# Reordering POOL's work, two operations changing engine, and 128-row v tiles in a windowed attention followed by a gated convolution

## The chip, the cores and the metric

The kernel runs on one core of a Trainium2 chip. The metric is the device time of one execution in microseconds. Before the change the median of three runs is 299.91 us (298.84 to 300.24).

## The reference

Batch 4, 8 heads, 768 positions, head size 64, all in float32. The first half is an attention in which a query sees the keys at a distance under 16 and, besides, one summary per block of 32 keys; the second half is a causal convolution of five taps that gates a projection.

```python
k_sum = k.reshape(B, H, nb, 32, D).max(axis=3)
v_sum = v.reshape(B, H, nb, 32, D).mean(axis=3)
scores_l = where(|i - j| < 16, q @ k.T / 8, -1e9)
scores_s = q @ k_sum.T / 8 + log(32)
a = softmax(concat(scores_l, scores_s))
x = a @ concat(v, v_sum)                 # B x 768 x 512
gate = sigmoid(sum_k conv_w[k] * x shifted by k)
out = (gate * (x @ w_val)) @ w_out
```

## The kernel before

A unit is a third of one batch's positions (256, four tiles of 64 queries) and four of the heads (two pairs); a group is two units and has all 512 channels of its positions. There are 24 units and 12 groups, three groups to a batch. The order of instructions is written out by hand and is the order in which each engine gets them. `step(s)` interleaves three units: it makes the scores of unit s, transposes the probabilities of unit s - 1, and multiplies unit s - 2 with v. The first four units and part of the fifth are written out singly ahead of the loop.

What a step gives each engine, in order:

- TensorE: a product from a queue (`proj`: an output product `out_mm`, L486), `mm_x` (probabilities times v, L393), `mm_s` (scores, L317), the first half of the transpositions `tp` (L373), a second product from the queue (a value product `val_mm`, L462), the second half of `tp`. In odd steps the value product reads the `xl` that the same step makes.
- VectorE: `snorm` (scores with mask and row maxima into `sn` and `nm`, L334), `taps` (the convolution, L437, and the first product of one head pair from group 3 on, L433), the reciprocal of the sums in `norm` (L356, L357), `val_ev` (`gf`, gate times value, L472), and in some steps `prep_k` (maxima `ks` of 32 keys, L126, and two copies of them into the key tile, L136).
- ScalarE: `out_ev` (`ob`), `xout` (`xh`, the part of x that TensorE's fast float form holds, L408, and `xf`, L409), `ginit` (first product of the convolution, x times the last tap, L422), the exponentials `exps`, the copies of the transposed tiles `pcopy` (`pts`, L377), `gate` (tanh, L445), and `gh` in `val_ev`.
- POOL: `xl` = `xf` - `xh` (L411), the halo of the next group (L294), `norm`'s multiplication of `p` by 1/sum in two halves (L360), `gl` = `gf` - `gh` in `val_ev` (L474), and in some steps `prep_v`, a tree of five additions that sums blocks of 32 columns of `vT` (L147).
- SyncE issues all transfers, in order.

`xl` and `gl` are the low parts of a split: a float32 product is made as three products of the fast form, `xh` with the high and the low part of the weights and `xl` with the high part. `split_w` makes the two parts of a weight tile (ScalarE's cast L247, POOL's subtraction L248) from a staged tile that `conv_w` fills (ScalarE L207, VectorE L209 and L210). For `wo` the staged tile `wst` has two buffers for four weight tiles.

`mm_x` reads a tile `v` of 120 rows, in which rows 16 to 27 and 92 to 103 are block means. `load_v` fetches the others from memory, from group 2 on in three pieces of 16, 64 and 16 rows, two transfers each; `fill_vs` puts the block means in with four transfers of 48 KB.

The trees and key maxima of batch b are made in the steps that `PREP_V` and `PREP_K` list: for b of 2 or 3, trees in steps 6b - 4 to 6b - 1 and maxima in steps 6b - 3 to 6b. Within a step `late_loads` puts both at the end.

Of the kernel before, what the change touches and what calls it, by code (L numbers as in the profile page):

```python
# [24 lines left out]
NTH = 3  # L25
# [16 lines left out]
NP = 2 * TPU  # L42
ACT_TAP_G = 3
LOADS = "k0 q0 m k1 q1 n0 i k2 q2 n1 k3 q3 n2 n3 v0 c Q w0 w1 w2 w3 v1 o0 o1 o2 o3"
UPB = NTH * NHP
LOAD_K = {1: (2, 2, 4, 5)}
PREP_K = {1: (4, 5, 5, 6)}
PREP_V = {1: (3, 4, 5, 5)}
for _b in range(2, B):
# [6 lines left out]
def tile_attention_then_gated_conv(  # L56
# [56 lines left out]
    def load_v(g):  # L113
        b, th = divmod(g, NTH)
        t = ld.tile([KW, TPU, DM], F32, tag="v", name=f"v_{g}")
        pieces = ((0, WIN), (OFF_O, OFF_B), (OFF_N, KW)) if g > 1 else ((0, KW),)
        for r0, r1 in pieces:
            for e in range(VP):
                nc.sync.dma_start(t[r0:r1, 2 * e : 2 * e + 2], vw[b, th, e, r0:r1])
        vtile[g] = t  # L120

    def prep_k(b, pr):
        t = ktile[b, pr]
        ks = wk.tile([P, NB], F32, tag="ks", name=f"ks_{b}_{pr}")
        own = t[:, OFF_O : OFF_O + STEP * NT].rearrange("p (t c) -> p t c", c=STEP)[:, :, :QT]
        nc.vector.tensor_reduce(  # L126
            ks.rearrange("p (t j) -> p t j", j=2),
            own.rearrange("p t (j c) -> p t j c", c=BLK),
            AX.X,
            ALU.max,  # L130
        )
        for half, n in ((0, NT // 2 + 1), (1, NT // 2)):
            c0 = OFF_A + half * STEP
            dst = t[:, c0 : c0 + 2 * STEP * n].rearrange("p (t c) -> p t c", c=2 * STEP)[:, :, :HB]
            src = ks[:, half * HB : half * HB + HB]
            nc.vector.tensor_copy(dst, src.unsqueeze(1).broadcast_to([P, n, HB]))  # L136

# [241 lines left out]
    def mm_x(u):  # L379
# [5 lines left out]
        for r in range(2):  # L385
            for i in range(TPU):
                for h in range(2):
                    c0 = (2 * hp + r) * P + h * D
                    dst = xp[h * D : (h + 1) * D, r, i * QT : (i + 1) * QT]
                    src = s["pts"][  # L390
                        :, TPU * r + 2 * (i // 2) + h, (i % 2) * QT : (i % 2 + 1) * QT
                    ]
                    nc.tensor.matmul(dst, v[:, i, c0 : c0 + D], src, start=True, stop=g > 0)  # L393
                    if g == 0:
                        nc.tensor.matmul(
                            dst, vblk[i % 2][:, c0 : c0 + D], src, start=False, stop=True
                        )

    def xout(u):
# [10 lines left out]
        if g:  # L410
            nc.gpsimd.tensor_tensor(  # L411
                G["xl"][:, prs, :], x[:, prs, HALO:], G["xh"][:, prs, :].bitcast(F32), ALU.subtract
            )

    def ginit(u):
# [4 lines left out]
        gt = s["gt"] = ps_g.tile([P, 2, SG], F32, tag="g", name=f"g_{u}")  # L420
        for r in range(2 if g < ACT_TAP_G else 1):
            nc.scalar.activation(  # L422
# [3 lines left out]
    def taps(u):  # L426
# [3 lines left out]
        for r in range(2):  # L430
            pr = 2 * hp + r
            if r and g >= ACT_TAP_G:
                nc.vector.tensor_scalar(  # L433
# [31 lines left out]
    def val_ev(g, cp, pp):  # L465
        G = group(g)
        cos = slice(2 * cp, 2 * cp + 2)
        if "gh" not in G:
# [4 lines left out]
        nc.scalar.copy(G["gh"][:, cos, :], gf)  # L473
        nc.gpsimd.tensor_tensor(  # L474
            G["gl"][:, cos, :], gf, G["gh"][:, cos, :].bitcast(F32), ALU.subtract
        )

# [35 lines left out]
    def early_loads(s):  # L513
        g, hp = divmod(s, NHP)
        if hp == 0 and 1 <= g < NG - 1:
            load_q(g + 1)
        for b in range(1, B):
            for i in range(NPR):
                if s == LOAD_K[b][i]:
                    load_k(b, i)  # L520
                    load_vT(b, i)

    def late_loads(s):
        g, hp = divmod(s, NHP)
        for b in range(1, B):
            for i in range(NPR):
                if s == PREP_K[b][i]:
                    prep_k(b, i)
                if s == PREP_V[b][i]:
                    prep_v(b, i)  # L530
            if s == b * UPB:
                prep_vs(b)
                fill_vs(b * NTH)
        if hp == NHP - 1 and 1 <= g < NG - 1:
            load_v(g + 1)
            if (g + 1) % NTH:
                fill_vs(g + 1)

    def step(s, late=lambda: None):
        u, t, x = s < NU, s - 1 < NU, s - 2 < NU  # L540
# [6 lines left out]
        if x:  # L547
# [3 lines left out]
            if hp == NHP - 1:  # L551
                queue_proj(g)
                if g + 1 < NG:
                    group(g + 1)
        if u:
            mm_s(s, 0)
            mm_s(s, 1)
# [8 lines left out]
        if u:  # L566
            exps(s, 1)
        if x:
            taps(s - 2)
# [60 lines left out]
    exps(2, 1)  # L630
    group(1)
    early_loads(2)
# [7 lines left out]
    ppv = [val_mm(0, 0), val_mm(0, 1)]  # L640
    split_w("wv", 0)
    split_w("wv", 1)
    taps(0)
    gate(0)
    ginit(1)
    norm(3)
    tp(2, 0)
    pcopy(2, 0)
    val_ev(0, 0, ppv[0])
    conv_w("wo", 0)  # L650
    conv_w("wo", 1)
    taps(1)
    tp(2, 1)
    pcopy(2, 1)
    gate(1)
    early_loads(3)
    split_w("wv", 2)
    val_ev(0, 1, ppv[1])
    split_w("wv", 3)
    late_loads(3)  # L660

    def late4():
        for k in range(2):
            split_w("wo", k)
# [6 lines left out]

    step(4, late4)
    step(5, late5)
    for s in range(6, NU + 2):
        step(s)
    while queue:
        proj()()

# [5 lines left out]
def _layout(q, k, v, moe_w_val, moe_conv_w, moe_w_out):  # L684
# [10 lines left out]
    vn[:, WIN : WIN + S] = v.transpose(0, 2, 1, 3).reshape(B, S, DM)  # L695
    vw = np.zeros((B, NTH, VP, KW, 2, DM), f)
    for t in range(NT):
# [52 lines left out]
```

## Time and profile before

| | before |
|---|---|
| median of 3 runs | 299.91 us (298.84 to 300.24) |
| the profiled execution | 299.31 us |
| its span | 297.5 us |
| TensorE, VectorE, ScalarE, POOL busy | 235.7, 211.6, 185.7, 148.6 us |
| granted TensorE clock, mean | 0.935 |

The span is the part of the execution that the trace covers, from the first to the last instruction. A row of a timeline has the start in us from the start of the span, the duration, the engine, the line, the operation, what it writes and reads, and in brackets the idle time before it and what ended that. Several equal instructions in a row are merged ("x8"). Each of an engine's instructions starts when the one before it is through and its inputs are there.

### The profile page before, as it was taken

What the parts mean: (1) busy time and instruction counts of PE and PEld (TensorE: products, weight loads), DVE (VectorE), ACT (ScalarE), POOL (GpSimd) and SP (SyncE); (2) the same over time, 40 slices, a digit from 0 to 9 for tenths busy, and PEclk for the clock granted to TensorE, in tenths of its full rate; (3) what the DMA queues carried; (4) which work ended last, traced back from release to release, by engine and by line L of the source; (5) the groups of instructions that cost most, each with busy time, mean ns of one, the idle gap of its engine ahead of it and who ended that gap; (6) DMA issues with size and microseconds to landing.
All of it is one profiled execution on the core that took longest, in us unless ns stands there. A gap on an engine that the chain in (4) does not pass through costs nothing.

```text
span 297.5 us, 7371 instructions
## 1 busy us (share of the span) xinstructions
PE 235.7 (79%) x2660; PEld 202.0 (68%) x2660; DVE 211.6 (71%) x740; ACT 185.7 (62%) x603; POOL 148.6 (50%) x187
## 2 busy tenths in 40 slices
PE   1268960726798995995998977986989989989895
PEld 0147840625497884884877866866868888878783
DVE  2887976599488677599498776598488876766600
ACT  2468956927088774774676873765757897774321
POOL 1150465883935547636832565665651465443330
PEclk9999996687599997998999997997999999999999
DMA  7999898516003986836106777824105452100112
GB/s 237 380 292 306 281 338 159 221 62 170 2 35 51 259 257 173 234 103 193 40 0 143 210 255 198 245 74 148 37 12 168 124 148 60 37 2 35 37 51 90
DMA packets 16848, 43.64 MB, mean 147 GB/s; under 512 B 2988, under 2 KB 3756, under 8 KB 16812
## 3 DMA queue, kind: packets, MB, share of 16 engines
q1 hardware_dynamic: 16812, 43.18, 48.5%
q8 instruction: 21, 0.34, 0.5%
q14 instruction: 15, 0.12, 0.2%
HBM read 34.71 MB, written 6.29 MB: 138 GB/s over the span
## 4 chain that ended last, share of the span: by engine, by line
DVE 34%; PE 33%; POOL 16%; DMA 8%; ACT 4%; issue 4%; SPq 0%; POOLq 0%; DVEq 0%; ACTq 0%
DVE g L437 18%; PE out L486 14%; PE val L462 10%; DVE sn L334 6%; POOL p L360 5%; DMA raw_wv<-in_wv_dram 4%; PE x L393 4%; PE s L317 4%; POOL gl L474 3%; POOL vT L147 3%; POOL xl L411 3%; DVE k L136 2%; PE pt L373 2%; DMA k<-in_kT_dram 2%; DMA qbd<-in_qT_dram 2%
## 5 line engine op out<-in xcount | busy, mean ns | idle before, releaser
L437 DVE SCALAR_TENSOR_TENSOR g<-xf,cwt,g 128x256 f32<-128x256 f32 x192 | 93.8, 489 | 13.1 <-ACT g L422 5.7
L360 POOL TENSOR_TENSOR p<-p,ri 128x480 f32<-128x480 f32 x48 | 46.5, 991 | 88.3 <-DVE ri L357 82.1
L348 ACT ACTIVATE p<-sn,nm 128x120 f32<-128x120 f32 x192 | 73.5, 389 | 19.4 <-DVE nm L334 19.4
L334 DVE CUSTOM_DVE_ANT_0 sn<-s,mask 128x120 f32<-128x120 f32 x192 | 41.0, 277 | 38.5 <-PE s L317 38.4
L486 PE MATMUL out<-wo,gh 128*128 128x512 f32 x192 | 53.6, 420 | 4.6 <-POOL wo L248 2.3
L462 PE MATMUL val<-xh,wv 128*128 128x256 f32 x352 | 54.1, 298 | 0.2
L462 PE MATMUL val<-xl,wv 128*128 128x256 f32 x176 | 32.8, 304 | 22.5 <-POOL xl L411 22.5
L462 PEld LDWEIGHTS val<-xh,wv 128*128 128x128 f32 x352 | 47.7, 200 | 0.8 <-ACT xh L408 0.6
L486 PEld LDWEIGHTS out<-wo,gh 128*128 128x128 f32 x192 | 36.1, 199 | 13.0 <-POOL wo L248 3.4
L373 PE MATMUL pt<-ident,p 128*120 128x128 f32 x192 | 32.8, 298 | 15.0 <-ACT pts L377 11.6
L462 PEld LDWEIGHTS val<-xl,wv 128*128 128x128 f32 x176 | 27.0, 208 | 24.1 <-POOL xl L411 24.1
L377 ACT COPY pts<-pt 120x512 f32<-120x512 f32 x48 | 27.6, 576 | 20.9 <-PE pt L373 20.9
L474 POOL TENSOR_TENSOR gl<-gf,gh 128x512 fp32r<-128x512 f32 x24 | 31.2, 1300 | 17.9 <-ACT gh L473 17.9
L317 PE MATMUL s<-k,qbd 64*64 64x120 f32 x768 | 28.4, 284 | 13.9 <-DVE k L136 8.5
L445 ACT ACTIVATE gt<-g 128x512 f32<-128x512 f32 x24 | 14.4, 599 | 36.5 <-DVE g L437 36.5
L348 ACT ACTIVATION_READ_ACCUMULATOR p<-sn,nm 128x1 f32 x192 | 37.1, 193 | 0.0
L373 PEld LDWEIGHTS pt<-ident,p 128*120 128x120 f32 x192 | 22.6, 146 | 19.8 <-POOL vT L147 11.1
L393 PEld LDWEIGHTS x<-pts,v 120*64 120x64 f32 x768 | 27.5, 143 | 10.2 <-issue 7.2
L317 PEld LDWEIGHTS s<-k,qbd 64*64 64x64 f32 x768 | 21.3, 141 | 17.3 <-DVE k L136 13.0
L393 PE MATMUL x<-pts,v 120*64 120x64 f32 x768 | 30.9, 231 | 1.5 <-ACT g L422 0.9
L147 POOL TENSOR_TENSOR vT<-vT 128x384 f32<-128x384 f32 (+3 forms) x48 | 27.9, 580 | 2.8
L411 POOL TENSOR_TENSOR xl<-xf,xh 128x512 fp32r<-128x512 f32 x22 | 28.2, 1281 | 0.3 <-ACT xf L409 0.2
(48 smaller groups left out, 273.9 us busy)
## 6 DMA issues: line engine op xcount, KB each, us to landing
k<-in_kT_dram SPq DMA_DIRECT2D x16, 478.0 KB
vT<-in_vT_dram SPq DMA_DIRECT2D x16, 384.0 KB
out_dram<-ob SPq DMA_DIRECT2D x24, 256.0 KB
qbd<-in_qT_dram SPq DMA_DIRECT2D x11, 512.0 KB
v<-in_vw_dram SPq DMA_DIRECT2D x20, 256.0 KB
v<-in_vw_dram SPq DMA_DIRECT2D x40, 64.0 KB
raw_wv<-in_wv_dram SPq DMA_DIRECT2D x4, 512.0 KB
raw_wo<-in_wo_dram SPq DMA_DIRECT2D x4, 512.0 KB
```

Source lines behind the costliest of these rows:

```text
L147: nc.gpsimd.tensor_tensor(dst, src[:, :, :n], src[:, :, n : 2 * n], ALU.add)
L317: nc.tensor.matmul(st[u]["sp"][64 * e : 64 * e + 64, h, c * KW : c * KW + KW], qbd[g % NQB][64 * h : 64 * h + 64, pr, i * QT : i * QT + QT ...
L334: nc.vector.tensor_tensor_reduce(s["sn"][:, n, :], s["sp"][:, h, c * KW : c * KW + KW], mask[:, mv, :], -1.0 / math.sqrt(D), 3.0e38, ALU.a ...
L348: nc.scalar.activation(s["p"][:, n, :], s["sn"][:, n, :], AF.Exp, bias=s["nm"][:, n : n + 1], scale=-1.0, accum_out=s["rs"][:, n : n + 1],)
L360: nc.gpsimd.tensor_tensor(s["p"][:, w], s["p"][:, w], ri[:, w].unsqueeze(2).broadcast_to([P, TPU, KW]), ALU.mult,)
L373: nc.tensor.transpose(s["pt"][:KW, i, :], s["p"][:, TPU * r + i, :], ident)
L393: nc.tensor.matmul(dst, v[:, i, c0 : c0 + D], src, start=True, stop=g > 0)
L411: nc.gpsimd.tensor_tensor(G["xl"][:, prs, :], x[:, prs, HALO:], G["xh"][:, prs, :].bitcast(F32), ALU.subtract)
L437: nc.vector.scalar_tensor_tensor(gt[:, r], x[:, pr, o : o + SG], cwt[:, pr, o : o + 1], gt[:, r], ALU.mult, ALU.add,)
L462: nc.tensor.matmul(pp[:, r], w, x, start=(n == 0), stop=(n == len(terms) - 1))
L474: nc.gpsimd.tensor_tensor(G["gl"][:, cos, :], gf, G["gh"][:, cos, :].bitcast(F32), ALU.subtract)
L486: nc.tensor.matmul(pp, x, w, start=(n == 0), stop=(n == len(terms) - 1))
```

## The change

The diff, cut to what does something. `prep_k`'s two copies go from VectorE to POOL. `load_v` fetches 128 rows in two transfers; the rows of the means, which memory now holds as zeros, are written over by `fill_vs`, which for the later groups of a batch moves from the end of a step to the beginning of the next one. The low part `gl` is no longer made in `val_ev` but by `val_low`, which a step calls behind `xout`; the trees (`trees`) follow there, ahead of `mm_s` and `norm`. The next group's halo is made in `xout`. The first products of the convolution are both on ScalarE, in group 1 both on VectorE. In the part that is written out, the `wv` splits go together, unit 1's taps move into step 4, and trees of batch 1 change their steps.

```diff
-ACT_TAP_G = 3
+VROWS = 128
+DVE_TAP_G = (1,)
-PREP_V = {1: (3, 4, 5, 5)}
+PREP_V = {1: (3, 3, 5, 5)}
     def load_v(g):
-        t = ld.tile([KW, TPU, DM], F32, tag="v", name=f"v_{g}")
-        pieces = ((0, WIN), (OFF_O, OFF_B), (OFF_N, KW)) if g > 1 else ((0, KW),)
-        for r0, r1 in pieces:
-            for e in range(VP):
-                nc.sync.dma_start(t[r0:r1, 2 * e : 2 * e + 2], vw[b, th, e, r0:r1])
+        t = ld.tile([VROWS, TPU, DM], F32, tag="v", name=f"v_{g}")
+        for e in range(VP):
+            nc.sync.dma_start(t[:, 2 * e : 2 * e + 2], vw[b, th, e])
...
-            nc.vector.tensor_copy(dst, src.unsqueeze(1).broadcast_to([P, n, HB]))
+            nc.gpsimd.tensor_copy(dst, src.unsqueeze(1).broadcast_to([P, n, HB]))
...
+        if hp == NHP - 1 and g + 1 < NG:
+            group(g + 1)                       # in xout, behind xl
...
-        for r in range(2 if g < ACT_TAP_G else 1):
+        for r in range(0 if g in DVE_TAP_G else 2):
...
-            if r and g >= ACT_TAP_G:
+            if g in DVE_TAP_G:
...
-        nc.gpsimd.tensor_tensor(
-            G["gl"][:, cos, :], gf, G["gh"][:, cos, :].bitcast(F32), ALU.subtract
-        )
+        lows.append((g, cos, gf))
+
+    lows = []
+
+    def val_low():
+        while lows:
+            g, cos, gf = lows.pop(0)
+            G = group(g)
+            nc.gpsimd.tensor_tensor(
+                G["gl"][:, cos, :], gf, G["gh"][:, cos, :].bitcast(F32), ALU.subtract
+            )
     def early_loads(s):
+        if hp == 1 and g >= 2 and g % NTH:
+            fill_vs(g)
...
+    def trees(s):
+        for b in range(1, B):
+            for i in range(NPR):
+                if s == PREP_V[b][i]:
+                    prep_v(b, i)
     def late_loads(s):
-                if s == PREP_V[b][i]:
-                    prep_v(b, i)
         if hp == NHP - 1 and 1 <= g < NG - 1:
             load_v(g + 1)
-            if (g + 1) % NTH:
-                fill_vs(g + 1)
-    def step(s, late=lambda: None):
+    def step(s, mid=lambda: None, late=lambda: None):
...
+        val_low()
         if u:
+            trees(s)
             mm_s(s, 0)
...
             exps(s, 1)
+        mid()
         if x:
             taps(s - 2)
...
     ppv = [val_mm(0, 0), val_mm(0, 1)]
-    split_w("wv", 0)
-    split_w("wv", 1)
+    for k in range(4):
+        split_w("wv", k)
     taps(0)
+    norm(3)
+    tp(2, 0)
+    conv_w("wo", 0)
+    conv_w("wo", 1)
+    pcopy(2, 0)
     gate(0)
     ginit(1)
-    norm(3)
-    tp(2, 0)
-    pcopy(2, 0)
-    val_ev(0, 0, ppv[0])
-    conv_w("wo", 0)
-    conv_w("wo", 1)
-    taps(1)
     tp(2, 1)
     pcopy(2, 1)
-    gate(1)
+    val_ev(0, 0, ppv[0])
     early_loads(3)
-    split_w("wv", 2)
-    val_ev(0, 1, ppv[1])
-    split_w("wv", 3)
     late_loads(3)
+    def mid4():
+        taps(1)
+        gate(1)
+        val_ev(0, 1, ppv[1])
     def late4():
+        trees(3)
         for k in range(2):
             split_w("wo", k)
         for k in range(2, 4):
             conv_w("wo", k)
...
-    step(4, late4)
-    step(5, late5)
+    step(4, mid4, late4)
+    step(5, late=late5)
```

## Rows read from the trace of the kernel before

**Rows 1.** The page's first part: busy time of each engine, its share of the span and its instructions.

```profile
PE 235.7 (79%) x2660; PEld 202.0 (68%) x2660; DVE 211.6 (71%) x740; ACT 185.7 (62%) x603; POOL 148.6 (50%) x187
```

**Rows 2.** Who waited for whom over the whole span: us in total, times, longest.

```profile
POOL p L360 <- DVE ri L357: 82.1, 19, 6.3
...
PE val L462 <- POOL xl L411: 22.5, 8, 5.7
...
PE s L317 <- DVE k L136: 8.5, 5, 2.6
```

**Rows 3.** The timeline of TensorE: the start of `mm_x` in steps 6, 9, 10, 11, 12, 15, 16, 17, 18, 21, 22, 23 and 24.

```profile
80.16 1.57 PE L393 MATMUL x<-pts,v 120*64 120x64 f32 x32
...
108.28 1.15 PE L393 MATMUL x<-pts,v 120*64 120x64 f32 x32
...
122.12 1.15 PE L393 MATMUL x<-pts,v 120*64 120x64 f32 x32
...
130.82 1.15 PE L393 MATMUL x<-pts,v 120*64 120x64 f32 x32
...
144.92 1.15 PE L393 MATMUL x<-pts,v 120*64 120x64 f32 x32
...
173.09 1.15 PE L393 MATMUL x<-pts,v 120*64 120x64 f32 x32
...
186.96 1.15 PE L393 MATMUL x<-pts,v 120*64 120x64 f32 x32
...
195.66 1.15 PE L393 MATMUL x<-pts,v 120*64 120x64 f32 x32
...
209.75 1.15 PE L393 MATMUL x<-pts,v 120*64 120x64 f32 x32
...
237.92 1.15 PE L393 MATMUL x<-pts,v 120*64 120x64 f32 x32
...
247.71 1.15 PE L393 MATMUL x<-pts,v 120*64 120x64 f32 x32
...
256.42 1.15 PE L393 MATMUL x<-pts,v 120*64 120x64 f32 x32
...
266.27 1.15 PE L393 MATMUL x<-pts,v 120*64 120x64 f32 x32
```

**Rows 4.** The timeline from the end of step 10 into step 11: POOL's instructions and the one of TensorE that follows. Four of a tree's five additions are merged into one row.

```profile
131.09 1.93 POOL L360 TENSOR_TENSOR p<-p,ri 128x480 f32<-128x480 f32 x2 [4.69 <-DVE ri L357]
...
132.98 1.28 POOL L474 TENSOR_TENSOR gl<-gf,gh 128x512 fp32r<-128x512 f32 x1
...
134.22 2.47 POOL L147 TENSOR_TENSOR vT<-vT 128x384 f32<-128x384 f32 x4
...
136.95 1.26 POOL L411 TENSOR_TENSOR xl<-xf,xh 128x512 fp32r<-128x512 f32 x1
...
138.27 0.50 PE L462 MATMUL val<-xl,wv 128*128 128x256 f32 x2 [3.56 <-POOL xl L411]
```

**Rows 5.** The same stretch: VectorE's first product, its two copies of key maxima, and ScalarE's `xf`.

```profile
128.04 0.49 DVE L433 TENSOR_SCALAR g<-xf,cwt 128x256 f32<-128x256 f32 x1
...
132.39 1.92 DVE L136 COPY k<-ks 128x84 f32<-128x84 f32 x2
...
133.01 0.60 ACT L409 COPY xf<-x 128x512 f32<-128x512 f32 x1
```

**Rows 6.** Busy time by stretch: the stretch, its length, busy us (instructions) of TensorE, its weight loads, VectorE, ScalarE and POOL, the granted clock, the share of the DMA engines and GB/s. First the opening of the kernel, then the stretch behind the wait of rows 4.

```profile
0.00:25.00 25.00, 10.53 (x149) 7.92 (x150) 16.09 (x61) 11.20 (x41) 6.61 (x18) 1.00 0.94 313
...
138.27:140.72 2.45, 2.45 (x15) 2.45 (x16) 2.27 (x7) 0.00 (x0) 0.12 (x1) 0.68 0.88 231
```

**Rows 7.** Groups of instructions by line and shape: count, busy us, mean ns of one, idle time before.

```profile
L247 ACT CAST wv<-wvf 128x512 fp32r<-128x512 f32 x4 | 2.3, 609 | 0.0
...
L168 POOL COPY vpad<-vpad 128x12 f32<-128x12 f32 x8 | 1.5, 193 | 13.7 <-DVE vpad L167 13.7
```

**Rows 8.** The timeline of step 21, which has no tree in front of it: ScalarE's `xf`, POOL's `xl`, TensorE behind it.

```profile
240.10 0.60 ACT L409 COPY xf<-x 128x512 f32<-128x512 f32 x1
...
241.31 1.27 POOL L411 TENSOR_TENSOR xl<-xf,xh 128x512 fp32r<-128x512 f32 x1
...
242.63 0.50 PE L462 MATMUL val<-xl,wv 128*128 128x256 f32 x2 [0.82 <-POOL xl L411]
```

**Rows 9.** The timeline of the first units: VectorE's first pair of copies, ScalarE behind the weights' transfer, step 4's `mm_x` and unit 1's taps, and from 56.42 on POOL and VectorE in steps 4 and 5.

```profile
4.82 0.31 DVE L136 COPY k<-ks 128x84 f32<-128x84 f32 x2
...
23.63 0.72 ACT L207 ACTIVATE sc_wv<-raw_wv 128x512 f32<-128x512 f32 x1 [1.89 <-DMA raw_wv<-in_wv_dram]
...
40.16 1.57 PE L393 MATMUL x<-pts,v 120*64 120x64 f32 x32 [0.51 <-DMA v<-vb]
...
42.94 4.16 DVE L437 SCALAR_TENSOR_TENSOR g<-xf,cwt,g 128x256 f32<-128x256 f32 x8
...
56.42 1.93 POOL L360 TENSOR_TENSOR p<-p,ri 128x480 f32<-128x480 f32 x2 [0.44 <-ACT gt L445]
...
59.62 1.48 DVE L209 TENSOR_SCALAR wst<-raw_wo 128x512 uint32<-128x512 uint32 x1 [3.38 <-POOL wo L248]
...
63.95 0.94 DVE L126 TENSOR_REDUCE ks<-k 128x24 f32<-128x768 f32 x1
...
75.18 2.50 POOL L248 TENSOR_TENSOR wo<-wst,wo 128x512 fp32r<-128x512 f32 x2
```

More of the change, by code (lines that the diff above doesn't have):

```diff
@@ L392, in mm_x @@
                     ]
-                    nc.tensor.matmul(dst, v[:, i, c0 : c0 + D], src, start=True, stop=g > 0)
+                    nc.tensor.matmul(dst, v[:KW, i, c0 : c0 + D], src, start=True, stop=g > 0)
                     if g == 0:
@@ L552, in step @@
                 queue_proj(g)
-                if g + 1 < NG:
-                    group(g + 1)
+        val_low()
         if u:
+            trees(s)
             mm_s(s, 0)
@@ L630, in tile_attention_then_gated_conv @@
     exps(2, 1)
-    group(1)
     early_loads(2)
@@ L676, in tile_attention_then_gated_conv @@
     while queue:
-        proj()()
+        ev = proj()
+        ev()
+        val_low()
 _INS = ["qT", "kT", "vT", "vw", "wv", "cw", "wo", "maskc", "identc"]
@@ L695, in _layout @@
     vn[:, WIN : WIN + S] = v.transpose(0, 2, 1, 3).reshape(B, S, DM)
-    vw = np.zeros((B, NTH, VP, KW, 2, DM), f)
+    vw = np.zeros((B, NTH, VP, VROWS, 2, DM), f)
     for t in range(NT):
```

## The prediction

> **What bounds the kernel now.** I read the page first. TensorE is busy 79% of the span, VectorE 71%, POOL 50% [rows 1]: an average that hides which engine ends which stage. The list of waits comes next, with what each engine stood still for [rows 2]. POOL idles 82.1 us, nearly all in front of one instruction, the multiplication of the exponentials by 1/sum, for which VectorE has to finish the taps first. And TensorE idles 22.5 us over eight waits, inside the value product, for `xl`, which POOL writes. So POOL has time to spare, and yet TensorE waits for it: a matter of order.
>
> The third view, TensorE's instructions in order, says what that costs [rows 3]. I take the start of `mm_x` as the beat. Step 10 lasts 122.12 to 130.82, 8.70 us, and so do steps 16 and 22. In such a step TensorE runs from one product into the next: 8.70 us is what a step costs when nothing holds it. Steps 9, 11, 15 and 17 last 13.84, 14.10, 13.87 and 14.09. Steps 21 and 23, which have no trees in front of them, last 9.79 and 9.85.
>
> The fourth view is POOL's timeline between steps 10 and 11 [rows 4]. Its order is `p` at 131.09, `gl` at 132.98, a tree from 134.22, `xl` at 136.95; at 138.27 TensorE goes on, after 3.56 us of idling. ScalarE had written `xf`, all that `xl` needs, from 133.01 on [rows 5]. So `xl` was ready to run at about 133.6 and stood 3.3 us behind `gl` and the tree, work that nobody needed yet. The 2.45 us behind it ran at a granted clock of 0.68, between the levels of 1.2 and 2.4 GHz [rows 6], so the 5.1 to 5.4 us that such a step loses are more than its idle time.
>
> **The steps of the loop, part by part.** *xl first, then gl, then tree.* In steps 9, 11, 15 and 17 `xl` now starts when `xf` is there. The other work goes where POOL idled in front of `p`. Does it fit? `xl` 1.26, `gl` 1.24 (132.98 to 134.22), a tree 2.73 (134.22 to 136.95), two `p` 1.89 (131.09 to 132.98) [rows 4]: 7.1 us, and with the copies below and a halo under 8.1, against 8.70 per step. `p` may also come late: its first half is needed only after the next `mm_s`. The four steps go to 8.70: 55.90 - 34.80 = **-21.1 us**.
>
> *Both first products on ScalarE* (from group 2 on). VectorE loses one instruction of 0.49 per step [rows 5], so tanh, `gf` and `gh`, then `ob`, `xh` and `xf` behind them on ScalarE, come about half a microsecond earlier. ScalarE gets one in its place behind `xf`, ahead of the exponentials; half as wide as its cast of 0.61 [rows 7], it is paid for by the half microsecond won. That is what steps 21 and 23 need: there `xf` starts at 240.10 and ends near 240.7, `xl` starts at 241.31 behind `gl`, and TensorE resumes at 242.63 after 0.82 [rows 8]. With `xl` at `xf`'s end, and `xf` 0.5 earlier, `xl` ends near 241.5, before TensorE stops at about 241.8. Both steps to 8.70: 19.64 - 17.40 = **-2.2 us**. The margin is 0.3 us, in the four tree steps too.
>
> *Maxima copied by POOL.* On VectorE a pair took 0.31 with POOL idle and 1.92 while POOL multiplied `p` [rows 5, 9]. VectorE is relieved; it isn't the bound. POOL's price is in no row. Nearest: its copy of 12 elements, 193 ns [rows 7]. From below, two of these, 0.4; from above, as much as two of the 128x512 subtractions, 2.5. The pair has 156 elements against 1024, so I take 0.6. [...] Where does the 0.6 lie? Behind `p`, which ends about 1.7 after `mm_x` (`p` starts 0.3 after it and lasts 1.9 [rows 3, 4], half a microsecond sooner in future), so the copies end around 2.3, when `xf` ends: hidden, with 0.3 to spare. Unhidden it would cost 0.6 in at most twelve steps. The pair of the last key tile of a batch is awaited by the next `mm_s`; VectorE's pair was awaited too (8.5 us of waits in all [rows 2]); I count no change. In the opening the four pairs come 0.3 later each, ahead of 1.89 us in which ScalarE waits for the weights [rows 9]: nothing, and up to 0.5 if that cover were gone.
>
> *v in 128 rows.* A group takes two loads in place of six, 256 KB more. The vs rows are now written over what the load wrote, so the fill must wait for the load; SyncE's queue holds the next q, k and vT loads and later out stores behind that wait. The fill goes out one step after the load and is read a step later, 8.7 us each: hidden. At the start the first group's tile grows by 64 KB ahead of the weights; at 313 GB/s [rows 6] that is 0.2 us, at a place where ScalarE waits for the weights' transfer [rows 9]: **+0.2**, counted with the first units.
>
> *Halo.* `group(g + 1)` is called from `xout`: same place on POOL behind `xl`. Nothing.
>
> *The end.* The last two units run the same order; the half microsecond from VectorE remains: **-0.5**.
>
> **The first units.** This is where I expect a loss. All four `wv` splits go ahead, so two casts of 0.61 [rows 7] lie on ScalarE in front of the copy that `mm_x(2)` needs: 40.16 becomes about 41.5 with the 0.2 above [rows 9]. `mm_x` and `mm_s` follow and the row maxima start 2.7 to 2.8 later, at 44.1. VectorE then does them (1.6), the eight taps of unit 1 (4.16 [rows 9]), waits 0.7 for tanh, `gf` 0.7, and unit 2's taps, now ten instructions of 0.52 because group 1's first products have moved to VectorE (5.2). `p` of step 4 starts near 57.1; before, 56.42, since there the taps stood ahead of the maxima. So far +0.7.
>
> Then POOL is the chain. Before: `p`, two `wo` splits, one tree, `xl`, `p` of step 5 when VectorE is ready, the other splits at 75.18, `mm_x` at 80.16 [rows 3, 9]. In between VectorE stood 3.38 us for the first `wo` split, because `wst` has two buffers. After: `p` 1.9 (59.0), two trees 5.5 (64.5), two splits 2.5 (67.0); only then can VectorE convert `wo` 2 and 3 and reduce the key tile. That took 59.62 to 64.9 for both conversions and the maxima [rows 9], of which I take 2.9 behind the second split (69.9). POOL's copies 0.6 (70.5), and only behind them `xl` with halo and `gl` 2.7 (73.2), two trees 5.5 (78.7), `p` 1.9 (80.6), splits 2.5 (83.1). TensorE's output product ended, and `mm_x` began, 80.16 - 77.68 = 2.5 after the last split (75.18 + 2.50): 85.6. That is **+5.4 us**, against 80.16. Bounds: 0 if the wait of VectorE is shorter than I lay it out, +10 if the conversions are contended again by POOL as at 59.62.
>
> **The sum.** The profiled execution took 299.31 us with a span of 297.5; the median shown is 299.91, 0.6 more, the runs spread over 1.4. 299.3 + 5.4 - 21.1 - 2.2 - 0.5 = 280.9; I say **281 us**. Half a percent, 1.5 us, is about what can be told from no change here.
>
> **The rivals.**
> *A: ScalarE, not POOL, then holds `xl`.* The 0.3 us margin is eaten by the second first product, and each of the six odd steps keeps the 1.1 us of steps 21 and 23. For it: there `xl` started only 0.6 after `xf` ended though no tree was in front of it [rows 8]. Against: `xf` itself should move up. 281 + 6.6 = 287.5.
> *B: the first units cost nothing.* The wait for two buffers overlaps more than I think, and `mm_x` of step 6 stays at 80.16. Against: POOL's own work in that chain sums to 23 us without VectorE's part. 281 - 5.4 = 275.5.
> *C, slower than before: POOL's copies are dear.* Place: between `p` and `xl`, in twelve steps of the loop. Each microsecond beyond 0.9 per pair holds `xl`, or `p` of the next step. The gain of 18.4 is gone at 0.9 + 18.4 / 12 = 2.4 per pair; at 3.0 the kernel takes 281 + 12 x 2.1 = 306. Against: 2.4 would be the price of two 128x512 subtractions for a seventh of the elements. For it: the destination is in runs of 12 with a repeated source, a form that POOL has in no row. A milder case is a pair at 1.9, VectorE's price beside POOL: 281 + 12 = 293. The Trainium skill has a mechanism for that (SBUF — State Buffer, section Who interferes with whom: VectorE's two-port modes and POOL shut each other out of a shared port pair); the pair at 0.31 and 1.92 agrees with it, and the maxima that will run beside the copies are not of that kind by the page.
> *D: the change doesn't shorten the tree steps*, because something ends just behind `xl`, such as the copy of `pt` that the second transposition needs, 0.2 to 0.3 before its turn in an undisturbed step: a stall of 0.2 in each of 17 steps is +3.4, 284. That stays within the forecast's own range.
>
> **How the numbers follow.** The forecast with D 0.63, its own range 277 to 285; A 0.14; B 0.10; first units worse, +10 in place of 5.4, 0.04; C mild 0.05, C slower than before 0.04. The range reaches to B below and A and the bad first units above, with a little for both: 274 to 289. Faster 0.94, same 0.02, slower 0.04.
>
> **What would show it.** Right: steps 9, 11, 15 and 17 near 8.7 from `mm_x` to `mm_x`; TensorE's 22.5 us of waits for `xl` down to a few; trees and `gl` in POOL's old idle time; VectorE's wait for the `wo` split up from 3.4 to about 8 us, and `mm_x` of step 6 near 85.6; POOL's pair of copies near 0.6. Wrong: copies over 0.9; `xl` starting at `xf`'s end and TensorE waiting all the same (A); `mm_x` waiting for the v fill; step 6 at 80 (B).

## The result: 278.7 us, and the profile after

| | before | after |
|---|---|---|
| median of 4 runs each, on one chip | 300.07 us (298.84 to 300.24) | 278.73 us (277.97 to 278.90) |
| ratio, with its 95% interval | | 0.929 (0.926 to 0.932) |
| the profiled execution, its span | 299.31, 297.5 us | 277.97, 276.2 us |

The forecast was 281 us, 274 to 289. The profiled execution is 2.9 us below the sum of 280.9. First the page's part on engines, of the changed kernel (busy us, share of the span, instructions), which answers to [rows 1]:

```profile
PE 231.2 (84%) x2660; PEld 198.4 (72%) x2660; DVE 187.9 (68%) x694; ACT 192.0 (70%) x617; POOL 155.6 (56%) x219
```

TensorE does its work in 4.5 us less busy time, and 16.8 us of its idle time are gone. The list of waits of the changed kernel over the whole span (us in total, times, longest) answers to [rows 2]:

```profile
POOL p L359 <- DVE ri L356: 53.0, 20, 8.5
...
POOL xl L410 <- ACT xf L408: 22.9, 20, 5.3
...
PE val L463 <- POOL xl L410: 11.1, 2, 10.2
...
DVE wst L208 <- POOL wo L247: 8.9, 1, 8.9
```

POOL's wait in front of `p` went from 82.1 to 53.0 us: the trees and `gl` lie there now. In front of `xl` POOL stands ready and waits 22.9 us for `xf`, where in before it waited 0.2. TensorE's wait for `xl` is down from eight times to two, and one of the two, 10.2 us, is in the first units. A stretch that begins with step 6's `mm_x` tells the loop and the end apart. These are all waits of TensorE's matmuls for another engine that the list names, before (from 80.1 us on):

```profile
PE val L462 <- POOL xl L411: 16.7, 7, 3.6
...
PE s L317 <- DVE k L136: 3.6, 3, 1.4
```

and after (from 85 us on):

```profile
PE val L463 <- POOL xl L410: 0.9, 1, 0.9
```

The second line of before is the one that the forecast passed over. The windows of the changed kernel are the first units from step 5's `mm_s` to step 6, the loop, and the end (length, busy time of each engine, granted clock, DMA share, GB/s); the fourth is the loop of before:

```profile
53.54:85.39 31.85, 14.86 (x78) 11.53 (x77) 16.16 (x44) 10.18 (x29) 22.32 (x37) 0.55 0.29 97
85.39:245.05 159.66, 159.66 (x1957) 140.09 (x1956) 122.69 (x495) 136.16 (x452) 103.41 (x138) 1.00 0.49 163
245.05:276.20 31.15, 26.48 (x205) 22.60 (x204) 9.77 (x20) 11.67 (x22) 9.25 (x8) 1.00 0.14 52
```

```profile
80.16:266.27 186.11, 166.64 (x1958) 145.51 (x1957) 141.82 (x529) 129.96 (x437) 100.59 (x125) 0.96 0.45 128
```

The loop lasts 159.66 us and TensorE is busy for 159.66 of them, at a granted clock of 1.00: no idle time is left in it that a better order could take. It lasted 186.11 with 166.64 busy at 0.96, so 19.5 us of the 26.4 won are idle time and 7.0 are the same instructions at a higher clock. The idle time is accounted for by the two lines of before: 16.7 for `xl`, of which 0.85 lie in the end, and 3.6 for the key tile's copies make 19.45. The starts of `mm_x`, in TensorE's timeline of the changed kernel (steps 6 to 12), answer to [rows 3]:

```profile
85.39 1.67 PE L392 MATMUL x<-pts,v 120*64 120x64 f32 x32
...
95.09 1.15 PE L392 MATMUL x<-pts,v 120*64 120x64 f32 x32
...
103.95 1.15 PE L392 MATMUL x<-pts,v 120*64 120x64 f32 x32
...
112.66 1.15 PE L392 MATMUL x<-pts,v 120*64 120x64 f32 x32
...
121.46 1.15 PE L392 MATMUL x<-pts,v 120*64 120x64 f32 x32
...
130.21 1.15 PE L392 MATMUL x<-pts,v 120*64 120x64 f32 x32
...
139.01 1.15 PE L392 MATMUL x<-pts,v 120*64 120x64 f32 x32
```

Put beside the sum of the forecast, with all step lengths taken so:

| part | before, us | after, us | difference | forecast |
|---|---|---|---|---|
| up to step 6's `mm_x` | 80.16 | 85.39 | +5.23 | +5.4 |
| steps 9, 11, 15, 17 | 55.90 | 35.17 | -20.73 | -21.1 |
| steps 21, 23 | 19.64 | 17.57 | -2.07 | -2.2 |
| steps 7, 13, 19 | 30.48 | 26.58 | -3.90 | 0 |
| the other nine steps | 80.09 | 80.34 | +0.25 | 0 |
| the end, from 266.27 and 245.05 on | 31.23 | 31.15 | -0.08 | -0.5 |
| span | 297.5 | 276.2 | -21.3 | -18.4 |

Three terms came as worked out, the end gave 0.1 of the 0.5, and one that was counted at nothing gave 3.9 us. How the order reads on POOL between steps 10 and 11, beside [rows 4], in POOL's timeline of the changed kernel (start, duration, and in brackets the idle time before it):

```profile
129.90 1.93 POOL L359 TENSOR_TENSOR p<-p,ri 128x480 f32<-128x480 f32 x2 [0.77 <-DVE ri L356]
131.78 0.44 POOL L135 COPY k<-ks 128x84 f32<-128x84 f32 x2
132.56 1.30 POOL L410 TENSOR_TENSOR xl<-xf,xh 128x512 fp32r<-128x512 f32 x1 [0.34 <-ACT xf L408]
...
133.99 1.29 POOL L483 TENSOR_TENSOR gl<-gf,gh 128x512 fp32r<-128x512 f32 x1
```

`xl` waits for ScalarE's `xf` alone and starts 2.35 us behind `mm_x`; in before it started 6.13 behind it. Only 0.77 us of POOL's idle time are left in front of this `p`.

### The profile page after: what moved, and what is told of

The parts are those of the page before. It is cut to its first block, busy times and chain, and to the rows that moved or that the text cites. A ratio compares the mean times of both kernels' runs of the same rounds, so it can differ in the third digit from the quotient of the medians.

```text
span 276.2 us, 7347 instructions
## 1 busy us (share of the span) xinstructions
PE 231.2 (84%) x2660; PEld 198.4 (72%) x2660; DVE 187.9 (68%) x694; ACT 192.0 (70%) x617; POOL 155.6 (56%) x219
## 4 chain that ended last, share of the span: by engine, by line
PE 66%; DVE 15%; POOL 7%; ACT 3%; issue 3%; DMA 3%; SPq 0%; DVEq 0%; POOLq 0%; ACTq 0%
PE out L495 23%; PE val L463 19%; PE s L316 8%; PE x L392 8%; DVE g L438 7%; PE pt L372 7%; POOL vT L146 2%; DVE sn L333 2%; DMA k<-in_kT_dram 2%; POOL p L359 2%; DVE wst L208 2%; DVE ks L125 1%; POOL xl L410 1%; POOL wo L247 1%; DMA vT<-in_vT_dram 1%
## 5 line engine op out<-in xcount | busy, mean ns | idle before, releaser
L495 PE MATMUL out<-wo,gh 128*128 128x512 f32 x192 | 52.3, 412 | 4.2 <-POOL wo L247 2.4
L463 PE MATMUL val<-xh,wv 128*128 128x256 f32 x352 | 52.6, 292 | 0.1
L463 PEld LDWEIGHTS val<-xh,wv 128*128 128x128 f32 x352 | 46.4, 195 | 0.6 <-ACT xh L407 0.3
L495 PEld LDWEIGHTS out<-wo,gh 128*128 128x128 f32 x192 | 35.0, 192 | 12.2 <-POOL wo L247 3.5
L410 POOL TENSOR_TENSOR xl<-xf,xh 128x512 fp32r<-128x512 f32 x22 | 28.4, 1290 | 23.0 <-ACT xf L408 22.9
L463 PE MATMUL val<-xl,wv 128*128 128x256 f32 x176 | 29.8, 290 | 11.1 <-POOL xl L410 11.1
L463 PEld LDWEIGHTS val<-xl,wv 128*128 128x128 f32 x176 | 25.2, 194 | 11.6 <-POOL xl L410 11.6
L146 POOL TENSOR_TENSOR vT<-vT 128x384 f32<-128x384 f32 (+3 forms) x48 | 27.3, 568 | 2.8
```

What stands on the lines that cost most here:

```text
L146: nc.gpsimd.tensor_tensor(dst, src[:, :, :n], src[:, :, n : 2 * n], ALU.add)
L410: nc.gpsimd.tensor_tensor(G["xl"][:, prs, :], x[:, prs, HALO:], G["xh"][:, prs, :].bitcast(F32), ALU.subtract)
L463: nc.tensor.matmul(pp[:, r], w, x, start=(n == 0), stop=(n == len(terms) - 1))
L495: nc.tensor.matmul(pp, x, w, start=(n == 0), stop=(n == len(terms) - 1))
```

## The experiments

Ten kernels, each beside runs of the kernel before on its own chip (medians of before: 299.6 to 300.5 us). Each asks about one part of the forecast: POOL's order gives the loop its gain (e5, e6, e8), the product moved to ScalarE gives the margin (e4), the copies (e3, e9) and the v tile (e7) give nothing, and the first units lose by the trees ahead of `wo`'s splits (e1, e2, e10). Step lengths are those of each kernel's profiled execution. Step 6 began at 84.2 to 86.4 us with the change and in e3, e4, e5 and e7, none of which touches the first units but for e7's loads and e3's copies; a difference of a microsecond there is not read as an effect.

| run | what differs | median, us | ratio to before, 95% |
|---|---|---|---|
| e1 | the change, no tree ahead of `wo`'s splits | 273.16 | 0.910 (0.906 to 0.914) |
| e2 | e1, and splits 2 and 3 a step earlier | 266.88 | 0.889 (0.885 to 0.893) |
| e3 | the change, copies back on VectorE | 278.03 | 0.927 (0.923 to 0.931) |
| e4 | the change, one first product back on VectorE | 282.12 | 0.941 (0.936 to 0.946) |
| e5 | the change, trees back at the end of a step | 288.71 | 0.963 (0.954 to 0.971) |
| e6 | the change, `gl` back behind `p` | 286.89 | 0.957 (0.950 to 0.964) |
| e7 | the change, v in pieces | 279.36 (one run) | |
| e8 | the kernel before, with POOL's new order in the loop | 275.24 | 0.919 (0.913 to 0.924) |
| e9 | e6 and e3 together | 288.17 | 0.960 (0.956 to 0.965) |
| e10 | e2, splits 2 and 3 behind `xl` | 266.75 | 0.890 (0.886 to 0.894) |

### POOL's order: e8, e5, e6

e8 takes the kernel before and gives it the order alone, `gl` from group 1 on and the trees from batch 2 on:

```diff
-        nc.gpsimd.tensor_tensor(
-            G["gl"][:, cos, :], gf, G["gh"][:, cos, :].bitcast(F32), ALU.subtract
-        )
+        lows.append((g, cos, gf))
+        if g == 0:
+            val_low()
...
-                if s == PREP_V[b][i]:
+                if s == PREP_V[b][i] and b == 1:
...
+        val_low()
         if u:
+            for b in range(2, B):
+                for i in range(NPR):
+                    if s == PREP_V[b][i]:
+                        prep_v(b, i)
```

> The kernel before with POOL's new order alone and only in the loop: `gl` behind the next `xl`, trees of batches 2 and 3 behind `gl`. First units, copies of the maxima, first products and v as before. If order were all: 300.0 - 21.1 - 2.2 = 276.7. If the other parts are needed to reach 8.7 us: the tree steps still lose 1 to 2 us each to VectorE's copies and first product, 282 to 288.

Measured: 275.24 us, less than the whole change. `mm_x` of step 6 starts at 79.66, the tree steps last 9.28 to 9.29, and steps 7, 13 and 19 last 8.77, 9.34 and 9.29. The order alone takes 23.0 us from the loop, the whole change 26.4; the other parts take some half a microsecond more from each odd step but step 7, which e4 gives to the first product, and lose 5.7 us in the first units against this run.

e5 puts batch 2's and 3's trees back to the end of a step:

```diff
-            trees(s)
+            if s < 6:
+                trees(s)
...
+        if s >= 6:
+            trees(s)
         if hp == NHP - 1 and 1 <= g < NG - 1:
             load_v(g + 1)
```

> The changed kernel with the trees of batches 2 and 3 back at the end of their steps, behind `p` and the copies of the maxima, so ahead of the next `xl`; `gl` stays behind `xl`. If the tree is the greater part of what held `xl` (2.73 of 3.97 us): `xl` of steps 9, 11, 15 and 17 ends 2 us after TensorE's turn, with a lower granted clock behind the wait about 3 us each, 290 to 291; even steps unchanged. If only both together held it: under 281.

Measured: 288.71 us; steps 9, 11, 15 and 17 last 10.84, 11.17, 10.79 and 12.68, the others are unchanged. In TensorE's timeline of e5 the value product of step 9 stops for `xl`, which now stands behind a tree:

```profile
116.75 0.40 PE L463 MATMUL val<-xl,wv 128*128 128x256 f32 x2
118.99 0.51 PE L463 MATMUL val<-xl,wv 128*128 128x256 f32 x2 [1.84 <-POOL xl L410]
```

That is a little under the 290 to 291 expected, with runs from 285.9 to 290.1. A tree alone costs 2.0 to 3.9 us per tree step, 10.3 in all, against 5.1 to 5.4 in before [rows 3]; `gl` alone, in e6, costs these four steps 2.7.

e6 leaves the trees and puts `gl` back into `val_ev`:

```diff
         lows.append((g, cos, gf))
+        if g:
+            val_low()
```

> The changed kernel with `gl` back in `val_ev`, behind `p` and ahead of the copies of the maxima and the next `xl` (from group 1 on). If 1.27 us of POOL's work ahead of `xl` are more than the margin: 0.5 to 1 us in each of the six odd steps from 9 to 23 in which `xl` is awaited, and steps 7, 13 and 19 wait 1.3 longer for their copies: 285 to 288. If `gl` fits into what POOL has left there: 279 to 280, and the gain is the trees' alone.

Measured: 286.89 us, as expected of a `gl` that is more than the margin. Steps 9 to 23, the odd ones without a batch's last copies, last 9.28 to 9.64, and steps 7, 13 and 19 last 10.13, 9.84 and 10.09. So `gl` behind `p` costs half a microsecond to a whole one in every odd step, and in steps 7, 13 and 19 it brings back 3.5 of the 3.9 us that before lost there. That these three steps hang on `gl` was not part of the forecast; e3 and e9 show how.

### The copies: e3, e9

e3 puts the pair of copies back on VectorE and leaves all else:

```diff
-            nc.gpsimd.tensor_copy(dst, src.unsqueeze(1).broadcast_to([P, n, HB]))
+            nc.vector.tensor_copy(dst, src.unsqueeze(1).broadcast_to([P, n, HB]))
```

> The changed kernel with the copies of the key maxima back on VectorE. By the prediction's step (VectorE isn't the bound, the copies are off the path but for the last pair of each batch): the three steps 7, 13 and 19 go from 8.9 back to about 10.3, and nothing else: 278.7 + 4 = 283. By the rival, that in the shorter step a pair of 1.9 beside POOL's `p` puts VectorE at sn 1.6, taps 4.2, reciprocal 0.35, gf 0.65, maxima 0.95, copies 1.9 = 9.7 against 8.8 us: each of the twelve steps with maxima costs 0.5 to 1 more, 287 to 291.

Measured: 278.03 us, the same within what can be told apart, and both expectations missed. Steps 7, 13 and 19 last 8.80, 8.79 and 8.79. The pair didn't take the 1.92 us that it took in before [rows 5], as the timeline of e3 at the head of step 13 shows:

```profile
147.54 1.93 POOL L359 TENSOR_TENSOR p<-p,ri 128x480 f32<-128x480 f32 x2 [3.55 <-DVE ri L356]
...
148.86 0.77 DVE L135 COPY k<-ks 128x84 f32<-128x84 f32 x2
```

The same place in before:

```profile
153.88 1.93 POOL L360 TENSOR_TENSOR p<-p,ri 128x480 f32<-128x480 f32 x2 [5.13 <-DVE ri L357]
...
155.19 1.90 DVE L136 COPY k<-ks 128x84 f32<-128x84 f32 x2
...
155.78 1.26 POOL L474 TENSOR_TENSOR gl<-gf,gh 128x512 fp32r<-128x512 f32 x1
...
157.14 0.64 PE L317 MATMUL s<-k,qbd 64*64 64x120 f32 x16 [1.35 <-DVE k L136]
```

In both the pair starts 0.6 us ahead of `p`'s end. In e3 nothing follows on POOL before `xl` at 150.62, and the pair ends at 149.63, 0.16 behind `p`. In before `gl` follows, the pair ends with `gl`, at 157.09, and TensorE's second half of `mm_s`, which reads the copies, starts then, after 1.35 us. Taken singly, the first copy of before lasts 0.69 us, to the end of `p`, and the second the rest. The Trainium skill has that rule (SBUF — State Buffer, section Who interferes with whom): a copy on VectorE can take the port pair that it shares with POOL, and whoever issues second waits for the whole of the other's instruction. The rows agree: each copy waits for one instruction of POOL, 0.69 and 1.21 us.

e9 asks for it directly, with `gl` behind `p` and the copies on VectorE:

> The changed kernel with gl moved back behind p (as in e6_gl_late) and the pair of copies back on VectorE (as in e3_kcopy_dve). It asks why the pair took 1.90 us on VectorE in the kernel before and 0.78 in e3. Theory 1 (VectorE's pair finishes when POOL's run of back-to-back instructions does): with gl directly behind p, a pair that starts in the last 0.7 us of p ends with gl or later, 1.8 to 2.0 us, as before; steps 7, 13, 19 and the odd steps stay at 9.3 to 10.3, and the time is that of e6 (286.9) within 2: 285 to 289. Theory 2 (the pair's length is its own, and something else made it 1.90 before): 0.77 to 0.80 as in e3, and since POOL is relieved of 0.44 ahead of xl the time is 3 to 4 below e6, 283 to 284.

Measured: 288.17 us, as theory 1 has it; VectorE's timeline of e9 at the head of steps 11 and 13:

```profile
135.28 1.92 DVE L135 COPY k<-ks 128x84 f32<-128x84 f32 x2
...
154.04 1.90 DVE L135 COPY k<-ks 128x84 f32<-128x84 f32 x2
```

The pair is back at 1.90 to 1.92, steps 7, 13 and 19 at 9.79, 10.33 and 10.29, which is before's 9.84, 10.31 and 10.33 again. With e6 (POOL's copies behind `gl`, 10.13, 9.84 and 10.09) this settles it: what the three steps lost in before they lost to `gl` behind `p`, whichever engine copies. Where `gl` is out of the way, either engine copies in time.

### The margin on ScalarE: e4

```diff
-        for r in range(0 if g in DVE_TAP_G else 2):
+        for r in range(0 if g in DVE_TAP_G else (2 if g < 3 else 1)):
...
-            if g in DVE_TAP_G:
+            if g in DVE_TAP_G or (r and g >= 3):
```

> The changed kernel with one first product per unit back on VectorE from group 3 on. By the margin of 0.3 us that the prediction gave `xl`: everything from tanh to `xf` 0.5 later, `xl` misses TensorE's turn by 0.2 to 0.3 in the eight odd steps from 9 to 23, each 0.3 to 0.6 longer: 281 to 283.5. By the rival that the product on ScalarE costs what the one on VectorE gives back: no difference, 278.7.

Measured: 282.12 us, and each odd step from 9 to 23 lasts 9.29 to 9.37 in place of 8.77 to 8.88. TensorE's timeline of e4, in step 9:

```profile
111.32 1.15 PE L392 MATMUL x<-pts,v 120*64 120x64 f32 x32
...
115.53 0.50 PE L463 MATMUL val<-xl,wv 128*128 128x256 f32 x2 [0.32 <-POOL xl L410]
```

VectorE's `gf` starts 0.03 us behind `mm_x` in e4 (111.35) and 0.49 ahead of it with the change (112.17 against 112.66). That half microsecond is what `xl` lacks here: 0.32 us of idling, and 0.5 us per step. `xl` came 0.52 us later against `mm_x` and TensorE stood 0.32, so the margin that the forecast put at 0.3 was 0.2, and the move of a 0.49 us instruction is worth about 4 us over eight steps. (The profiled execution is only 2.8 above that of the change since its step 6 begins at 84.17, 1.2 earlier.)

### The v tile: e7

```diff
-        for e in range(VP):
-            nc.sync.dma_start(t[:, 2 * e : 2 * e + 2], vw[b, th, e])
+        pieces = ((0, WIN), (OFF_O, OFF_B), (OFF_N, KW)) if g > 1 else ((0, KW),)
+        for r0, r1 in pieces:
+            for e in range(VP):
+                nc.sync.dma_start(t[r0:r1, 2 * e : 2 * e + 2], vw[b, th, e, r0:r1])
```

> The changed kernel with v loaded in pieces as before (120 rows for the first two groups, then 16, 64 and 16 rows); the fill stays where the change put it. The prediction gave the larger tiles +0.2 us ahead of the weights; in the trace ScalarE got the first weights 1.1 us earlier instead (22.54 against 23.63). If the 128-row tiles do that: back at about 23.6, `p` of step 4 unchanged near 57, since it hangs on VectorE. If the earlier weights come from elsewhere (VectorE and POOL being ahead in the opening): 22.5. The whole within 0.5 us of the changed kernel either way.

Measured: 279.36 us, one run; the loop's steps last what they last with the change, 8.7 to 8.9. Its step 6 begins at 86.35, a microsecond later than with the change, and the whole is 0.6 above it, where at most 0.5 was expected; no loss and no gain that one run could tell.

### The first units: e1, e2, e10

e1 takes the first two trees of batch 1 from ahead of `wo`'s splits and puts them where POOL idled 8.52 us, ahead of step 4's `p`:

```diff
-PREP_V = {1: (3, 3, 5, 5)}
+PREP_V = {1: (4, 4, 5, 5)}
...
     def late4():
-        trees(3)
         for k in range(2):
```

> The changed kernel, in which the first two trees of batch 1 run in step 4 ahead of `norm(4)` (where POOL idled 8.5 us, 48.45 to 56.96) instead of behind it and ahead of the `wo` splits. If the 5.2 us lost in the first units are POOL's chain through the trees: `p` of step 4 stays at 57, VectorE's wait for the first `wo` split falls from 8.9 to about 3.4 us, `mm_x` of step 6 goes from 85.4 to 80.0, the kernel from 278.7 to 273.3, the loop unchanged at 159.7. If the loss lies elsewhere (the split's two buffers, unit 1's taps, the copies on POOL): step 6 stays above 84 and the time at 278.

Measured: 273.16 us, `mm_x` of step 6 at 79.75, VectorE's wait for the `wo` split 3.4 us, all as expected. e2 goes on and does the last two splits at the end of step 4 and not of step 5:

```diff
         for k in range(2, 4):
             conv_w("wo", k)
-
-    def late5():
         for k in range(2, 4):
             split_w("wo", k)
...
-    step(5, late=late5)
+    step(5)
```

> As the run before, and the last two `wo` splits are put at the end of step 4, ahead of the key maxima and of `xl`, instead of behind the second pair of trees and `p` of step 5. By the chain: the output product of step 6 no longer waits for POOL, only the value product for `xl` (about 67); `mm_x` of step 6 near 76, the kernel near 269.5. If something else stands behind the splits (the next `mm_s` for the copies of the maxima, which stay behind `p` of step 5): `mm_s` of step 6 near 77 to 80 all the same, the kernel 271 to 273.

Measured: 266.88 us, `mm_x` of step 6 at 74.66, better than either expectation. The loop is the same. This is 11.9 us below the changed kernel. TensorE's timeline of the change, of e1 and of e2, where the value product of step 5 goes on, with the output product's stop in e1 and its undisturbed run in e2:

```profile
71.69 0.79 PE L463 MATMUL val<-xl,wv 128*128 128x256 f32 x2 [10.24 <-POOL xl L410]
```

```profile
66.05 0.80 PE L463 MATMUL val<-xl,wv 128*128 128x256 f32 x2 [4.78 <-POOL xl L410]
...
76.08 2.02 PE L495 MATMUL out<-wo,gh 128*128 128x512 f32 x3 [2.42 <-POOL wo L247]
```

```profile
64.59 1.22 PE L463 MATMUL val<-xh,wv 128*128 128x256 f32 x4 [4.79 <-ACT xh L407]
...
67.42 0.80 PE L463 MATMUL val<-xl,wv 128*128 128x256 f32 x2 [1.19 <-POOL xl L410]
...
71.29 2.51 PE L495 MATMUL out<-wo,gh 128*128 128x512 f32 x8
```

In e2 the value product waits for `xh` too, which ScalarE makes behind the casts of `wo`, and goes on 1.4 later than in e1. Step 6 all the same starts 5.1 earlier: there the output product finds `wo` ready, and doesn't wait behind two trees and `p`. e10 tries to get ahead of that too, with the key maxima ahead of `wo`, and the splits behind `xl` and `gl`:

```diff
         val_low()
+        low()
         if u:
             trees(s)
...
-        late()
         if u:
             late_loads(s)
+        late()
...
-    step(5)
+    step(5, low=low5)
```

where `low5` has the two splits that e2 has at the end of `late4`.

> On top of e2_trees_wo: step 4's key maxima go ahead of the wo work, and wo's last two splits go behind step 5's xl and gl in place of ahead of them. In e2's trace ScalarE's xh of that step stands behind two wo casts that wait for VectorE (63.96 in place of about 59.1), and xl starts at 66.11 behind the splits and the copies. If that chain sets the first units, xl starts at about 61.6, the splits end at about 67, the output product follows them and mm_x of step 6 begins near 70.5 in place of 74.66: 262 to 264 us. Rival: VectorE's conversions for these splits, now beside xl, halo and gl on POOL, are drawn out by 3 to 4 us, the splits end where they did, and the time stays at 266 to 267.5. The loop's steps are as in the changed kernel in either case.

Measured: 266.75 us, no different from e2. `xl` started at 61.48 and the splits ended at 67.88, near what was expected, but `mm_x` of step 6 came at 73.33 and not 70.5, and the step behind it lasted 10.11 against 9.66. VectorE's conversions, of which now two more ran beside POOL's subtractions, `xl` and `gl`, in e10:

```profile
60.33 1.49 DVE L208 TENSOR_SCALAR wst<-raw_wo 128x512 uint32<-128x512 uint32 x1 [2.94 <-POOL wo L247]
61.92 1.56 DVE L209 SCALAR_TENSOR_TENSOR wst<-sc_wo,wst 128x512 uint32<-128x512 uint32 x1
63.41 0.42 DVE L208 TENSOR_SCALAR wst<-raw_wo 128x512 uint32<-128x512 uint32 x1
63.93 1.58 DVE L209 SCALAR_TENSOR_TENSOR wst<-sc_wo,wst 128x512 uint32<-128x512 uint32 x1
```

took 5.2 us from the first to the last, against 3.4 in e2 (60.00 to 63.40). ScalarE's casts of `wo` waited for them, its copies of the transposed tiles came behind the casts, and TensorE stood 1.87 us for these until 68.21. Then the output product itself ran slower:

```profile
68.97 3.50 PE L495 MATMUL out<-wo,gh 128*128 128x512 f32 x8
...
80.46 2.11 PE L495 MATMUL out<-wo,gh 128*128 128x512 f32 x8
```

It took 3.50 us at a granted clock of 0.54, against 2.51 at 0.81 in e2, where TensorE had run without a stop since 67.42. The rival's mechanism was there, with 1.8 us and not 3 to 4; the rest went into the late copies, the slower product, and a step 6 in which the scores waited 0.69 us for POOL's key copies (0.25 in e2).

## Why the prediction was right, and where it was not

**The tree steps (-21.1, measured -20.7).** Right in amount and reason. `xl` was late for work that nobody needed yet, and TensorE paid with idle time and with clock. e5, e6 and e8 show it from three sides.

**Steps 21 and 23, and the margin (-2.2, measured -2.1).** Right. `xl` ended ahead of TensorE's stop, and e4 shows what the move of the first product gives it: without the half microsecond the odd steps from 9 on lose 0.5. The margin was 0.2 and not 0.3. Rival A, in which ScalarE holds `xl` all the same, didn't come: in the loop TensorE waits for `xl` no more.

**The first units (+5.4, measured +5.2).** The chain on POOL came step by step:

```profile
56.96 1.93 POOL L359 TENSOR_TENSOR p<-p,ri 128x480 f32<-128x480 f32 x2 [8.52 <-DVE ri L356]
...
64.35 2.48 POOL L247 TENSOR_TENSOR wo<-wst,wo 128x512 fp32r<-128x512 f32 x2
69.97 0.44 POOL L135 COPY k<-ks 128x84 f32<-128x84 f32 x2 [3.14 <-DVE ks L125]
70.37 1.27 POOL L410 TENSOR_TENSOR xl<-xf,xh 128x512 fp32r<-128x512 f32 x1
...
80.41 2.50 POOL L247 TENSOR_TENSOR wo<-wst,wo 128x512 fp32r<-128x512 f32 x2
```

The forecast had `p` at 57.1, the splits' end at 67.0, `xl` at 70.5 and the last splits at 80.6. VectorE's wait for the `wo` split was 8.85 us against about 8. e1 took the trees away and 5.6 us went. The loss is there, so rival B is out. But the way to 57.1 was wrong in its first steps, and two errors cancelled: that 0.7 of the 5.4 came out is luck. `mm_x(2)`, step 4's, was to slip from 40.16 to 41.5 by two casts and the v tile, and started at 40.34. The two casts did come ahead of the copy that it reads, but tanh and unit 1's first products, which lay ahead of that copy in before, now follow it; ScalarE's timeline of before and of the change:

```profile
37.44 0.93 ACT L422 ACTIVATE g<-x,cwt 128x256 f32<-128x256 f32 x2
38.29 0.59 ACT L377 COPY pts<-pt 120x512 f32<-120x512 f32 x1
```

```profile
34.76 2.17 ACT L246 CAST wv<-wvf 128x512 fp32r<-128x512 f32 x4
...
38.24 0.59 ACT L376 COPY pts<-pt 120x512 f32<-120x512 f32 x1 [0.17 <-PE pt L372]
```

The weights came no later either: ScalarE's first scaling of them started at 22.54 in place of 23.63. The v tile isn't the reason (22.50 in e7, with v in pieces), and e8, which has the opening of before, has 22.77, so most of that is the spread between runs. What held VectorE's row maxima until 44.17, where the forecast had 44.1, was its own work: the conversions of `wo` 0 and 1 beside POOL's `wv` subtractions, which end at 40.59, and `p` behind them, to 43.11, in VectorE's timeline of the change:

```profile
38.14 1.33 DVE L208 TENSOR_SCALAR wst<-raw_wo 128x512 uint32<-128x512 uint32 x1
39.57 1.56 DVE L209 SCALAR_TENSOR_TENSOR wst<-sc_wo,wst 128x512 uint32<-128x512 uint32 x1
41.06 1.21 DVE L208 TENSOR_SCALAR wst<-raw_wo 128x512 uint32<-128x512 uint32 x1
42.37 1.28 DVE L209 SCALAR_TENSOR_TENSOR wst<-sc_wo,wst 128x512 uint32<-128x512 uint32 x1
```

**The copies and the steps behind them (0, measured -3.9).** This is the term that was mis-sized. The step that failed is "VectorE's pair was awaited too (8.5 us of waits in all [rows 2]); I count no change." Of the waits of TensorE for that pair in [rows 2] three lie in the loop and sum to 3.6 us, at the head of steps 7, 13 and 19. Filtered to the stretch from 80 us on, the view would have shown them beside `xl`'s. The forecast looked at which engine copies, and put the pair's 1.92 us down to POOL's `p`. Its own rows say otherwise: the pair of [rows 5] starts at 132.39, 0.63 before `p` ends, and ends with `gl` [rows 4]. The length of the pair was set by what POOL had queued behind `p`, so moving `gl`, counted as part of the tree steps and of steps 21 and 23 alone, freed these three as well (e3, e6, e9). POOL's pair was estimated at 0.6 and measured at 0.44 (256 and 244 ns); rival C's threshold of 0.9 wasn't near. Of the twelve steps that C counts in the loop nine lie there, the others in the first units, so its 2.4 per pair should have been 2.9. e3 shows that the move itself is worth nothing here.

**The end (-0.5, measured -0.1).** In the end there are no scores and no exponentials. VectorE's taps wait there for both of ScalarE's first products: 2.98 us, and they start 3.22 us behind `mm_x` (255.99 against 252.77); in before, with one product to wait for, they started 2.78 behind it (276.82 against 274.04). The half microsecond taken from VectorE is spent waiting, and the last wait for `xl` stays, 0.87 against 0.85.

**v and halo (0.2 and 0).** e7 shows nothing against the zero in the loop; the 0.2 is below what a run can tell. The halo was not tried by itself.

**Rival D** would have shown as stalls of 0.2 in the loop. TensorE is busy for the whole of it, and the even steps kept their 8.70 to 8.75 (steps 12 and 18, 9.1 to 9.2 in both kernels).

## What to carry to other kernels

When one engine's order changes, list who waits for whom in the stretch concerned, and ask of every row, the small ones too, whether its length is its own or that of a neighbour's queue: here three waits, 3.6 us together, vanished when another engine's instruction was moved. Test the parts of a bundle singly: the order alone came to 275.2 us and the whole bundle to 278.7, since the rest lost more at the start than it won in the loop. And where an engine with idle time later in the loop is the chain at the start, put what the chain awaits first there too, and the work that isn't needed yet into the engine's idle time: two trees moved into such time and two splits moved forward gave 11.9 us.

## What the runs showed of the hardware

- A pair of small copies on VectorE took 0.31 us with POOL idle [rows 9], 0.77 to 0.80 in the last 0.6 us of POOL's `p`, and 1.90 to 1.93 when POOL went from `p` straight into `gl`. In these rows the copy that starts while POOL is in an instruction ends with it, and the next copy ends with POOL's next instruction.
- On POOL the same pair took 0.43 to 0.45 us wherever it ran with the change and in e6; its two copies have means of 256 and 244 ns.
- VectorE's conversions of 128x512 words, two instructions each, took 0.42 and 0.69 us with POOL idle (67.82 and 68.35 with the change), and 1.2 to 1.6 each beside POOL's subtractions and `p`. So POOL's order also sets the time that they take: 5.2 us for two in e10, 3.4 in e2.
- The output product's eight matmuls took 3.50 us in e10's first units at a granted clock of 0.54, 2.51 in e2's at 0.81, and 2.11 in e10's step 6 at 1.00, the level of 2.4 GHz. In the window that ends with step 6 the change, with TensorE busy for 14.86 of 31.85 us, has a granted clock of 0.55, between the levels of 1.2 and 2.4 GHz, and in the loop 1.00.
